# Output products of an MLP in halves of 256 columns, and the tiles of h begun 192 bytes past a multiple of 512

## The chip, the cores and the metric

The kernel runs on one core of a Trainium2 chip. The metric is device time of one execution in microseconds (us), the median of several runs.

## The reference, cut to what matters

A retention layer (attention without a softmax, with a decaying lower triangle) gives x of 2304 tokens by 512. Two MLPs follow.

```python
attn_out = _attn_ref(q, k, v)                       # 4 batches, 8 heads, 576 tokens, 64
x = attn_out.transpose(0, 2, 1, 3).reshape(2304, 512)
h = np.maximum(x @ moe_w_in, 0.0)                   # 512 -> 2048
x = (h * h) @ moe_w_out                             # 2048 -> 512
g = x @ moe2_w_gate                                 # 512 -> 1536
x = (g / (1 + np.exp(-g)) * (x @ moe2_w_val)) @ moe2_w_out
```

The change touches `(h * h) @ moe_w_out`, the output product of the first MLP.

## The kernel before, in words

**Precision.** Every operand of an MLP product is kept as two fp32r tiles, a high part and the rest. `three` (L235 to L237) issues a product as three matmuls, high·high, high·low and low·high, all added up in PSUM. Each matmul is preceded by its own load of 128 by 128 weights (LDWEIGHTS, the rows of PEld).

**Blocks of tokens.** `BLOCKS` cuts the first MLP's tokens into five blocks j of 512, 256, 512, 512 and 512. Blocks 0 and 1 (`PLAIN_BLOCKS = 2`) are computed plainly: `mlp1_h` makes one 128-row piece f of h (of 16) in the bank `hps`, `mlp1_act` makes max(h,0) squared and its two parts in a tile `h`, and `mlp1_y` multiplies that with the output weights and adds it to four PSUM tiles `acc` (e = 0 to 3). The retention of the later tokens is put between the pieces of these two blocks. Blocks 2 to 4 take the input product in Strassen's manner, two pieces f at a time (`mlp1_s`, step p of 8): seven products of 256 columns, six matmuls each, moving operand `xb`, into the banks `gv` and `hps`; between them stand the output products of the step before, as pieces `y` (one e of one f: three matmuls of 512 columns, rows acc<-h,w). A step orders its work as product 0, 1, two pieces, 2, 3, two pieces, 4, 5, two pieces, 6, two pieces. After that comes the second MLP (`mlp2_gv`, rows gv<-xc,w of 384 columns, and its output pieces, rows with 128x256 and `at`).

**Order of the work.** `Plan` writes the order of each engine's instructions from costs given by hand; an operation's cost is a number beside the function that emits it. TensorE's operations are chained in program order (`pe`). The queue of DMA issues is SP's.

**Where tiles lie.** The pools are stacked in SBUF in the order of the code; pools named `pad...` shift what follows. Before the change the pool `hp` (two slots of 4096 bytes) begins at a multiple of 512 bytes, and `shift(n)` moves a tile of h with under 512 columns, that of block 1, by 48 elements (192 bytes). The tiles x of block 1 and `xb` begin 192 bytes past a multiple of 512, as their pads have it; those of x of block 0, of `xc` and of the weights begin at a multiple of 512.

Of the kernel before, what the change touches and what calls it, by code (L numbers as in the profile page):

```python
# [10 lines left out]
F32 = mybir.dt.float32  # L11
F32R = mybir.dt.float32r
# [12 lines left out]
NF1, NF2 = F1 // 128, F2 // 128  # L25
# [11 lines left out]
PLAIN_BLOCKS = 2  # L37
# [4 lines left out]
HALF1 = 256  # L42
# [150 lines left out]
def kernel(ctx: ExitStack, tc: tile.TileContext, units, qtab, tab, w1, w2, out):  # L193
# [15 lines left out]
    wp = ctx.enter_context(tc.tile_pool(name="wp", bufs=1, side="right"))  # L209
    wstack = ExitStack()  # L210
    wa = wstack.enter_context(tc.tile_pool(name="wa", bufs=NA, side="right"))
    ctx.enter_context(tc.tile_pool(name="pad2", bufs=1)).tile([128, 224], F32, name="pad2")
    hp = ctx.enter_context(tc.tile_pool(name="hp", bufs=2))
    io = ctx.enter_context(tc.tile_pool(name="io", bufs=3))
    sp = ctx.enter_context(tc.tile_pool(name="sp", bufs=1))
    cv = ctx.enter_context(tc.tile_pool(name="cv", bufs=1))
# [16 lines left out]
    def three(ps, ws, xs, first, last, onto=False):  # L233
        (wh, wl), (xh, xl) = ws, xs
        nc.tensor.matmul(ps, lhsT=wh, rhs=xh, start=first, stop=False, skip_group_check=onto)  # L235
        nc.tensor.matmul(ps, lhsT=wh, rhs=xl, start=False, stop=False, skip_group_check=onto)  # L236
        nc.tensor.matmul(ps, lhsT=wl, rhs=xh, start=False, stop=last, skip_group_check=onto)  # L237
# [3 lines left out]
    def pe(us, fn, deps=(), fill=None):  # L241
        o = do("PE", us, fn, [*deps, pe_last[0]])
        o.fill = fill
        pe_last[0] = o
        return o
# [254 lines left out]
    def shift(n):  # L500

        return 48 if n < 512 else 0
# [178 lines left out]
    def out_cols(f, e):  # L681
        t, at = Wt[f // 2 * 2 + 1], f % 2 * 512 + e * 128
        return [t[:, a, at:at + 128] for a in range(2)]

    Hs, accs = {}, {}
# [30 lines left out]
    def mlp1_act(j, f):  # L716
        n = BLOCKS[j][1] * C
        i = at1[j, f]
        k = n / 512
        st = {}  # L720
        on_act = True

        def relu():
            st["r"] = io.tile([128, n], F32, tag="io", name="r")
            nc.scalar.activation(out=st["r"], in_=banks[0][:, :n], func=ACTF.Relu)

        def square():
            if on_act:
                nc.scalar.activation(out=st["r"], in_=st["r"], func=ACTF.Square)
            else:  # L730
                nc.vector.tensor_tensor(out=st["r"], in0=st["r"], in1=st["r"], op=ALU.mult)

        def hi():
            t = hp.tile([128, 2 * n + shift(n)], F32R, tag="h", name="h")
            Hs[j, f] = t[:, shift(n):].rearrange("p (a n) -> p a n", a=2)
            nc.scalar.copy(out=Hs[j, f][:, 0], in_=st["r"])

        def lo():
            nc.vector.tensor_tensor(out=Hs[j, f][:, 1], in0=st["r"], in1=Hs[j, f][:, 0].bitcast(F32), op=ALU.subtract)

        a = do("ACT", 0.17 + 0.43 * k, relu, [h_op[j, f], hlo_op.get(order1[i - 1]) if i else None], -3)
        relu_op[j, f] = a
        if on_act:
            b = do("ACT", 0.19 + 0.43 * k, square, [a], -2)
        else:
            b = do("DVE", 0.16 + 0.53 * k, square, [a], -2)
        c = do("ACT", 0.19 + 0.43 * k, hi, [b, y_op.get(order1[i - 2]) if i > 1 else None], -2)
        hlo_op[j, f] = do("DVE", 0.16 + 0.53 * k, lo, [c], -2, lock=True)

    io_users, io_alloc = [], []  # L750

    def mlp1_y(j, f, apart=False):

        n = BLOCKS[j][1] * C

        def go(es=range(KC)):
            ht = Hs[j, f]
            for e in es:
                if f == 0:
                    accs.setdefault(j, {})[e] = pacc.tile([128, n], F32, tag="acc", name="acc")  # L760
                three(accs[j][e], out_cols(f, e), [ht[:, a] for a in range(2)], f == 0, f == NF1 - 1)

        def piece(e):
            def emit():
                free = [acc_free[j - 1][e]] if f == 0 and j else []
                y_op[j, f] = y_op[j, f, e] = pe(3 * n * MM, lambda: go([e]), [hlo_op[j, f], *free])
                if e == KC - 1 and f == NF1 - 1:
                    mlp1_save(j)
            return emit

        if apart:
            return [piece(e) for e in range(KC)]
        if f == NF1 - 1:
            for e in range(KC):
                piece(e)()
            return
        y_op[j, f] = pe(12 * n * MM, go, [hlo_op[j, f], w1_done[f // 2 * 2 + 1], *(acc_free.get(j - 1, ()) if f == 0 else ())])
# [745 lines left out]
    for b in range(N2):  # L1523
# [13 lines left out]
        for f in range(NF2):  # L1537
# [9 lines left out]
            n = len(mine)  # L1547
# [94 lines left out]
```

## Time and profile before

| | |
|---|---|
| runs, median (lowest to highest) | 863.67 us (862.26 to 865.38), 3 runs |
| the profiled execution's own time | 866.6 us |
| its span, first to last instruction | 864.8 us |
| mean granted clock of TensorE, share of full speed | 0.996 |
| TensorE busy | 853.8 us (99%) |
| VectorE, ScalarE, GpSimd busy | 628.0, 506.7, 134.7 us |

The profile shows one execution. PE is TensorE's matmuls and PEld its weight loads, DVE is VectorE, ACT ScalarE, POOL GpSimd, SP the queue that issues DMAs. A matmul's duration runs from its start to its last result, and the next one starts before that; so the time that matmuls cost is read from start to start (called the pitch below), not from durations.

### The profile page before, as it was taken

The page shows a single profiled execution, that of the slowest core. Times are in us where ns is not written, and L with a number is a line of the kernel's source. Part 1 is how long each engine was busy: PE and PEld are TensorE (multiplying, and loading weights), DVE is VectorE, ACT ScalarE, POOL GpSimd, SP SyncE. Part 2 cuts the span into 40 slices and gives each one's busy share as a digit, 9 for nine tenths or more (in the row PEclk, how much of TensorE's full clock was granted, in tenths as well). Part 3 has the DMA queues.
Part 4 walks back from the last instruction along what each step waited for, and adds up shares of the span by engine and source line. Part 5 has one row for each costly group of instructions (what it writes and reads, how often), then busy time and mean ns, then how long its engine had stood idle before and what let it go on. Part 6 is the DMA issues. An engine that isn't in the chain of part 4 may idle for free.

```text
span 864.8 us, 15867 instructions
## 1 busy us (share of the span) xinstructions
PE 853.8 (99%) x5990; PEld 804.0 (93%) x5990; DVE 628.0 (73%) x1034; ACT 506.7 (59%) x994; POOL 134.7 (16%) x141
## 2 busy tenths in 40 slices
PE   8999999999999999999999999999999999999998
PEld 6878888989999999999998999999999999999998
DVE  5799987646677857785788778588666688656675
ACT  3577774437877877887887444365333355333353
POOL 3121127651223022212310201000000000000000
PEclk9899999999999999999999999999999999999999
DMA  9587879999989789969899898978867788776782
GB/s 369 206 329 268 305 268 315 387 379 301 316 297 329 267 288 346 315 233 329 281 342 385 300 402 296 392 259 308 318 227 263 261 261 281 276 260 223 267 265 74
DMA packets 113084, 254.83 MB, mean 295 GB/s; under 512 B 8560, under 2 KB 67696, under 8 KB 103664
## 3 DMA queue, kind: packets, MB, share of 16 engines
q1 hardware_dynamic: 113008, 253.82, 83.5%
q8 instruction: 47, 0.77, 0.4%
q14 instruction: 29, 0.24, 0.1%
HBM read 195.59 MB, written 58.20 MB: 293 GB/s over the span
## 4 chain that ended last, share of the span: by engine, by line
PE 92%; DMA 5%; ACT 1%; DVE 1%; issue 0%; SPq 0%; DVEq 0%
PE gv L235 13%; PE gv L237 13%; PE gv L236 13%; PE acc L237 7%; PE acc L236 7%; PE acc L235 7%; PE acc L1285 4%; PE acc L1287 4%; PE acc L1286 4%; PE hps L235 4%; PE hps L237 4%; PE hps L236 4%; PE sc L577 1%; DMA raw<-w 1%; DMA qk<-units 1%; DMA w<-ws 1%
## 5 line engine op out<-in xcount | busy, mean ns | idle before, releaser
L235 PE MATMUL gv<-xc,w 128*128 128x384 f32 x504 | 169.4, 336 | 0.2 <-ACT u L1133 0.2
L237 PE MATMUL gv<-xc,w 128*128 128x384 f32 x504 | 168.9, 335 | 0.0
L236 PE MATMUL gv<-xc,w 128*128 128x384 f32 x504 | 168.7, 335 | 0.0
L236 PE MATMUL acc<-h,w 128*128 128x512 f32 (+1 forms) x320 | 117.3, 367 | 0.0
L237 PE MATMUL acc<-h,w 128*128 128x512 f32 (+1 forms) x320 | 117.3, 367 | 0.0
L235 PE MATMUL acc<-h,w 128*128 128x512 f32 (+1 forms) x320 | 117.3, 367 | 0.0
L453 POOL TENSOR_TENSOR f<-f 128x256 f32<-128x256 f32 x72 | 61.9, 859 | 274.2 <-DVE cw L410 181.5
L235 PEld LDWEIGHTS gv<-xc,w 128*128 128x128 f32 x504 | 94.6, 188 | 1.3 <-ACT u L1133 0.6
L236 PEld LDWEIGHTS gv<-xc,w 128*128 128x128 f32 x504 | 94.6, 188 | 0.1
L237 PEld LDWEIGHTS gv<-xc,w 128*128 128x128 f32 x504 | 94.6, 188 | 0.0
L1287 PE MATMUL acc<-w,at 128*128 128x256 f32 x288 | 81.0, 281 | 0.0
L1285 PE MATMUL acc<-w,at 128*128 128x256 f32 x288 | 80.9, 281 | 0.0
L1286 PE MATMUL acc<-w,at 128*128 128x256 f32 x288 | 80.9, 281 | 0.0
L237 PEld LDWEIGHTS acc<-h,w 128*128 128x128 f32 x320 | 60.1, 188 | 10.0
L235 PE MATMUL gv<-xb,w 128*128 128x256 f32 x238 | 67.1, 282 | 0.0
L237 PE MATMUL gv<-xb,w 128*128 128x256 f32 x238 | 66.8, 281 | 0.0
L236 PE MATMUL gv<-xb,w 128*128 128x256 f32 x238 | 66.8, 281 | 0.0
L236 PEld LDWEIGHTS acc<-h,w 128*128 128x128 f32 x320 | 60.1, 188 | 6.4
L235 PEld LDWEIGHTS acc<-h,w 128*128 128x128 f32 x320 | 60.1, 188 | 6.4
L927 DVE TENSOR_TENSOR h<-g,h 128x256 fp32r<-128x256 f32 x96 | 47.9, 499 | 19.1 <-ACT h L923 18.2
L1145 DVE TENSOR_TENSOR m<-gv,m 128x384 f32<-128x384 f32 x36 | 20.1, 558 | 53.5 <-PE gv L237 53.5
L1133 ACT COPY m<-gv 128x384 f32<-128x384 f32 x72 | 34.5, 479 | 40.7 <-PE gv L237 40.2
(174 smaller groups left out, 2094.9 us busy)
## 6 DMA issues: line engine op xcount, KB each, us to landing
w<-wdS SPq DMA_DIRECT2D x36, 1024.0 KB, 5.5
raw<-w SPq DMA_DIRECT2D x34, 1024.0 KB, 7.5
w<-wdP SPq DMA_DIRECT2D x36, 768.0 KB, 7.3
w<-ws SPq DMA_DIRECT2D x94, 256.0 KB, 5.0
w<-wdOP SPq DMA_DIRECT2D x54, 256.0 KB, 5.4
w<-wdOS SPq DMA_DIRECT2D x18, 768.0 KB, 7.5
ws<-cw SPq DMA_DIRECT2D x16, 512.0 KB, 8.5
wdS<-cw SPq DMA_DIRECT2D x12, 512.0 KB, 6.3
```

What stands on the lines that cost most here:

```text
L235: nc.tensor.matmul(ps, lhsT=wh, rhs=xh, start=first, stop=False, skip_group_check=onto)
L236: nc.tensor.matmul(ps, lhsT=wh, rhs=xl, start=False, stop=False, skip_group_check=onto)
L237: nc.tensor.matmul(ps, lhsT=wl, rhs=xh, start=False, stop=last, skip_group_check=onto)
L453: nc.gpsimd.tensor_tensor(out=w[:, o], in0=w[:, x], in1=w[:, y], op=op)
L577: nc.tensor.matmul(s[h][:, p], lhsT=A[c][r, p, 1], rhs=A[c][r, p, 0], start=True, stop=True)
L927: nc.vector.tensor_tensor(out=t[:, 1, half], in0=st[key][:, half], in1=t[:, 0, half].bitcast(F32), op=ALU.subtract)
L1133: nc.scalar.copy(out=st[name], in_=late[bank][:, :HALF])
L1145: nc.vector.tensor_tensor(out=st["m5"], in0=late["MA"][:, :HALF], in1=st["m5"], op=ALU.add)
L1285: nc.tensor.matmul(ps, lhsT=ah, rhs=wh, start=product not in ONTO and q == 0 and off == 0, stop=False, skip_group_check=True)
L1286: nc.tensor.matmul(ps, lhsT=ah, rhs=wl, start=False, stop=False, skip_group_check=True)
L1287: nc.tensor.matmul(ps, lhsT=al, rhs=wh, start=False, stop=q == NQ - 1, skip_group_check=True)
```

## The change

Where block j is 2, 3 or 4, each output piece of three matmuls over 512 columns becomes six over 256: three for the first half of the columns, then three for the second, with the same weights, into the two halves of the same PSUM tile. And pads move the pool `hp` by 320 bytes: its tiles now begin 192 bytes past a multiple of 512, for every block; the shift inside block 1's tile is dropped, so that block 1 lies as it did, while what stands behind `hp` keeps its place. The costs that `Plan` reads stay the same.

```diff
-    ctx.enter_context(tc.tile_pool(name="pad2", bufs=1)).tile([128, 224], F32, name="pad2")
+    ctx.enter_context(tc.tile_pool(name="pad2", bufs=1)).tile([128, 144], F32, name="pad2")
     hp = ctx.enter_context(tc.tile_pool(name="hp", bufs=2))
+    ctx.enter_context(tc.tile_pool(name="pad7", bufs=1)).tile([128, 80], F32, name="pad7")
...
         def hi():
-            t = hp.tile([128, 2 * n + shift(n)], F32R, tag="h", name="h")
-            Hs[j, f] = t[:, shift(n):].rearrange("p (a n) -> p a n", a=2)
+            Hs[j, f] = hp.tile([128, 2, n], F32R, tag="h", name="h")
...
-                three(accs[j][e], out_cols(f, e), [ht[:, a] for a in range(2)], f == 0, f == NF1 - 1)
+                if j < PLAIN_BLOCKS:
+                    three(accs[j][e], out_cols(f, e), [ht[:, a] for a in range(2)], f == 0, f == NF1 - 1)
+                    continue
+                for lo in range(0, n, HALF1):
+                    half = slice(lo, lo + HALF1)
+                    three(accs[j][e][:, half], out_cols(f, e), [ht[:, a, half] for a in range(2)], f == 0 and not lo, f == NF1 - 1, True)
```

## Rows read from the trace of the kernel before

**Rows 1.** The page, first part: busy us (share of the span) and instructions.

```profile
PE 853.8 (99%) x5990; PEld 804.0 (93%) x5990; DVE 628.0 (73%) x1034; ACT 506.7 (59%) x994; POOL 134.7 (16%) x141
```

**Rows 2.** Waits of TensorE, whole span: first and last of ten.

```profile
PE hps L236 <- DVE x L649: 1.9, 1, 1.9
...
PE gv L235 <- ACT u L1133: 0.2, 1, 0.2
```

**Rows 3.** Windows by stage: us, busy time and instructions of each engine, clock, DMA.

```profile
223.50:301.00 77.50, 77.50 (x488) 70.26 (x487) 59.02 (x100) 64.31 (x141) 14.37 (x16) 1.00 0.89 304
...
379.00:457.00 78.00, 78.00 (x496) 70.91 (x495) 58.29 (x97) 62.05 (x139) 17.44 (x20) 1.00 0.88 302
457.00:475.00 18.00, 17.76 (x93) 16.15 (x93) 14.72 (x25) 12.68 (x21) 1.68 (x2) 1.00 0.98 383
```

**Rows 4.** TensorE's groups by form, started in or running into 223.52 to 456.84.

```profile
L235 PE MATMUL acc<-h,w 128*128 128x512 f32 x182 | 70.8, 389 | 0.0
...
L235 PE MATMUL gv<-xb,w 128*128 128x256 f32 x218 | 61.3, 281 | 0.0
L235 PE MATMUL hps<-xb,w 128*128 128x256 f32 x88 | 24.7, 281 | 0.0
...
L235 PE MATMUL gv<-xb,sx 128*128 128x256 f32 x2 | 0.6, 281 | 0.0
```

**Rows 5.** Timeline of TensorE: start us, us, engine, line, operation.

```profile
224.21 0.39 PE L235 MATMUL acc<-h,w 128*128 128x512 f32 x1
...
225.57 0.28 PE L235 MATMUL hps<-xb,w 128*128 128x256 f32 x1
```

**Rows 6.** The same view, end of block 1 and start of block 2.

```profile
212.44 0.28 PE L237 MATMUL acc<-h,w 128*128 128x256 f32 x1
...
218.22 0.28 PE L237 MATMUL gv<-xb,w 128*128 128x256 f32 x1
218.39 0.39 PE L235 MATMUL gv<-xb,w 128*128 128x256 f32 x1
...
219.20 0.28 PE L235 MATMUL hps<-xb,w 128*128 128x256 f32 x1
...
219.54 0.28 PE L235 MATMUL hps<-xb,w 128*128 128x256 f32 x1
```

**Rows 7.** The same view, end of block 0's last output product, block 1's first pieces.

```profile
149.28 0.39 PE L237 MATMUL acc<-h,w 128*128 128x512 f32 x1
149.51 0.28 PE L235 MATMUL hps<-x,w 128*128 128x256 f32 x1
```

**Rows 8.** The same view, retention between two pieces of block 1.

```profile
155.04 0.28 PE L237 MATMUL acc<-h,w 128*128 128x256 f32 x1
155.16 1.05 PE L604 MATMUL xs<-qt,state 128*128 128x128 f32 x8
...
158.72 0.38 PE L235 MATMUL hps<-x,w 128*128 128x256 f32 x1
...
159.53 0.28 PE L235 MATMUL hps<-x,w 128*128 128x256 f32 x1
...
160.21 0.28 PE L235 MATMUL acc<-h,w 128*128 128x256 f32 x1
```

**Rows 9.** Timeline of VectorE in a step of block 2.

```profile
245.23 0.42 DVE L901 TENSOR_TENSOR g<-hps,m 128x256 f32<-128x256 f32 x1 [0.76 <-PE hps L237]
```

**Rows 10.** Timeline of TensorE in the same step.

```profile
247.03 0.28 PE L235 MATMUL hps<-xb,w 128*128 128x256 f32 x1
```

**Rows 11.** The queue's waits: us in total, times, longest.

```profile
SPq L1098 <- PE gv L237: 207.4, 67, 7.8
SPq L841 <- PE gv L237: 50.6, 50, 6.0
```

**Rows 12.** The chain that ended last, at the start of the second MLP.

```profile
458.09 0.02 ACT m L1133
...
463.08 0.39 ACT u L1133
```

**Rows 13.** TensorE's groups by form, whole span.

```profile
L237 PE MATMUL gv<-xc,w 128*128 128x384 f32 x504 | 168.9, 335 | 0.0
...
L1287 PE MATMUL acc<-w,at 128*128 128x256 f32 x288 | 81.0, 281 | 0.0
...
L237 PE MATMUL acc<-h,w 128*128 128x256 f32 x64 | 17.7, 277 | 0.0
```

**Rows 14.** Timeline of TensorE in the second MLP's last quarter.

```profile
770.93 0.28 PE L1285 MATMUL acc<-w,at 128*128 128x256 f32 x1
...
772.30 0.34 PE L235 MATMUL gv<-xc,w 128*128 128x384 f32 x1
```

## The prediction

> **What bounds the kernel now.** I read the page first: TensorE is busy for 853.8 of 864.8 us, VectorE for 628.0 [rows 1]. Then what TensorE waits for: ten waits in the whole span, none over 1.9 us, the last of them 0.2 us at the start of the second MLP [rows 2]. Then the windows, since an average over stages can hide one with another limit: in blocks 2 to 4, the stretch that the change is about, TensorE is busy for the whole of 77.5 and 78 us at a granted clock of 1.00 (its upper level, 2.4 GHz), with DVE at about 59 and ACT at about 64 [rows 3]. So in this stretch the time is the number of matmuls times their pitch, and nothing else. Last the timeline, to get pitches, because this is where the surprise lies.
>
> The reader is to see two pitches for one and the same kind of matmul. The six 512-column matmuls from 224.21 to 225.57 take 1.36 us, 226.7 ns each [rows 5]. In the stretch from 223.52 to 456.83, three lines with 182 of them each make 546; the 256-column ones on `xb` are three lines of 218 on gv, of 88 on hps, and 12 with `sx` (two triples on gv as shown, two on hps), 930 in all [rows 4]. 233.31 us less 546 x 226.7 ns leaves 109.5 us, or **117.8 ns** each. But just ahead of it, from 212.44 to 218.22, 51 matmuls of 256 columns follow one another, block 1's output pieces and block 2's first `xb` products mixed, in 5.78 us: **113.3 ns** each, exactly half of a 512-column one [rows 6]. Same shapes, same weights pool, same clock: 4.5 ns differ.
>
> What came before decides which pitch it is. Behind the last 512-column matmul of block 0 the 48 matmuls of block 1 from 149.51 on run 47 steps to 155.04, 117.7 ns each [rows 7, 8]. Then the retention work comes between; the first matmul after it takes twice its time, the pitch settles within six, and from 159.53 to 160.21 six take 0.68 us, 113.3 ns [rows 8]. A pause at 218.22 does the same: behind it the pitch is at 113.3 again from 219.20 on [rows 6]. So a 512-column matmul with its operand at a multiple of 512 sets the slow pitch, the slow pitch then keeps itself up, and a pause clears it. Since 223.52, where block 2's first 512-column piece starts, one such piece stands in every step, and the slow pitch never leaves.
>
> **The change, part by part.**
>
> *The halves.* 576 matmuls (4 e, 16 f, 3 blocks, 3 each) become 1152 of half the length: at 113.3 ns the pair takes 226.6 ns against 226.7, no change; at 117.8 ns it takes 235.6, 8.9 more. Each brings a weight load; at the 113.3 ns of rows 6 every matmul has one of its own, so that it lies hidden under the matmul before it. If that cover were gone the pitch would rise; the nearest row to that is the slow 117.8.
>
> A rule of the Trainium skill speaks against the split: the page TensorE: Matmul & The Clock Gate, section Back-to-back issue gap, gives N / 2.4 + 2.5 ns, so a fixed 2.5 ns for every matmul. By it 576 more of them would cost 1.4 us (an estimate from that page), and a 256-column one would always take the same. The rows disagree with both: two at 113.3 make one at 226.7 [rows 5, 6], which leaves no fixed part, and there are two pitches.
>
> *What the halves remove.* From block 2 on no 512-column matmul is left until the second MLP. Block 2 is entered at the fast pitch [rows 6]; what interrupts it there, pauses, leads back to the fast one. Then the 930 `xb` matmuls run at 113.3: 930 x 4.5 = **4.2 us less**. Bounds: 0 (all stay at 117.8) to 4.2.
>
> *The 192 bytes.* For blocks 2 to 4 they put the halves of h where `xb` and block 1's h lie, whose mix ran at 113.3 [rows 6]. In block 0 192 matmuls of 512 columns now begin there too, a form that the trace doesn't have. A gain is excluded, as 226.7 is already twice the fastest 256-column pitch; a loss is bounded by the slow surcharge, 192 x 4.5 = 0.9 us. I take 0, since at 256 columns this place shows the fast pitch. If the place and not the length is what sets the slow pitch, block 1's 48 slow matmuls gain 48 x 4.4 = 0.2 us more.
>
> *Behind the stretch.* The last 30 pieces' matmuls run among the 384-column ones of the second MLP, where the slow pitch rules (below): 30 x 8.9 = 0.3 us more at most; I take 0.2.
>
> *Does the gain reach the end?* Three things could be late when TensorE comes 4 us sooner. The evictions inside a step: VectorE's add for product 4 runs 245.23 to 245.65 and its bank is next written at 247.03 [rows 9, 10], 1.4 us of room, against 27 ns that each product gets shorter. The loads: SP waits for TensorE to free their places, 207.4 us in all at L1098 and 50.6 at L841 [rows 11]; they are set off by TensorE and come sooner with it. And ACT at the start of the second MLP, the one place where the chain leaves TensorE: from 458.09 to 463.47 it runs through ACT [rows 12]. But that piece begins with the copy of the second MLP's own first product, so it moves along whole. DMA is at 0.98 of its time there [rows 3]; I count no loss, and up to 1 us for the range. Nothing is moved past a queue: `Plan` reads the same costs, so the order of every engine is the old one.
>
> The sum: -4.2 + 0.2 = -4.0 us. Against the profiled execution, 864.8 us of span and 1.8 around it, 866.6 - 4.0 = 862.6. That execution is 2.9 above the median of the runs, so the median becomes 863.67 - 4.0 = **859.7 us**.
>
> **Rivals.**
>
> *Slower: the slow pitch stays.* If the pitch is slow for another reason than the 512-column pieces, say the alternation of banks or of products with y pieces, the 930 gain nothing and 576 pairs pay 8.9 ns: +5.1 us, 868.8. For it: output pieces of the second MLP, all 256 columns, average 281 ns of duration, block 1's 277, so they are slow there nearly throughout [rows 13] though no 512-column matmul is near. Against it: they stand among 384-column ones, and rows 6 show the very mix of blocks 2 to 4 running fast. It decides where more than 46% of the stretch's 2022 short matmuls (930 and 1092) are slow: all of them slow cost 9.1 us, now 4.2 are paid.
>
> *The pitch changes back and forth.* If something besides pauses and long matmuls sets the slow pitch now and then, a third to a half of the matmuls stay slow: -1.2 to +0.4 us, 862.5 to 864.0, within 0.3% (2.6 us, about what a measurement of this kernel can tell from no change). Waits that eat the gain at the second MLP end there too.
>
> *A cost per matmul.* If each of the 576 extra matmuls pays something of its own, the rows bound it at 0 (two at 113.3) and 8.9 ns (two at 117.8). It takes 576 times that from the 4.0: at a third of the upper bound, 3 ns, -2.3 us remain, 861.4; from 7 ns on nothing does. Against it stands that 226.7 is twice 113.3. This is the rule of the Trainium skill named above (TensorE: Matmul & The Clock Gate, Back-to-back issue gap), by which alone, with no gain on `xb`, the time would be 863.67 + 1.4 = 865.1.
>
> *More: the second MLP gets fast too.* If the fast pitch lives on there, its output pieces, x288 on three lines on acc alone [rows 13], would save 864 x 4.5 = 3.9 us more: 855.8. Once they do run fast, from 770.93 to 772.30, 12 in 1.37 us [rows 14]. Against it: the 384-column matmuls before it set the slow pitch as the long ones do.
>
> **How the numbers follow.** The forecast 0.65, the slow pitch 0.12, back and forth 0.11, a cost per matmul 0.07, more 0.05. The forecast alone spans 858.6 (the 0.2 of block 1, and 0.9 for the spread of the runs) to 861.6 (0.9 in block 0, 1 behind the stretch). The range leaves out the slow rival whole (0.12) and most of "more" (0.04): 857.2 to 866.0, the upper end being back and forth with a spread of 1.9 us for the runs. Faster by over 0.3%: 0.60 of the forecast, all of "more", a third of the cost per matmul: 0.67. Within 0.3%: the rest of the forecast, of the cost and of back and forth: 0.20. Slower: the slow rival and 0.01 of back and forth: 0.13.
>
> **What the profile would show.** Right: durations of gv<-xb and hps<-xb near 277 instead of 281, 1152 more short acc<-h rows at 277, about 229 us from the first output piece of block 2 to the first gv<-xc, and TensorE without a new wait. Wrong: xb at 281 and acc<-h with it (slow); pitches that switch inside the stretch; hps<-x and acc<-h of block 0 above 389 ns (place); or a wait of TensorE at the second MLP that grew by microseconds.

## The result, and the profile after

The changed kernel takes **868.95 us** (median of 9 runs, 866.07 to 872.75) against 863.78 for the kernel before beside it; the ratio is 1.0067, 95% interval [1.0052, 1.0082]. It is slower, by about the 5.1 us of the rival *the slow pitch stays*. Its profiled execution took 871.61 us, with a span of 869.8 against 864.8.

The page first, its busy part, then the waits of TensorE (us in total, times, longest), then two windows by stage:

```profile
PE 858.2 (99%) x6566; PEld 829.4 (95%) x6566; DVE 626.1 (72%) x1034; ACT 507.5 (58%) x994; POOL 135.6 (16%) x141
```

```profile
PE hps L237 <- DVE x L650: 1.9, 1, 1.9
...
PE gv L236 <- ACT u L1138: 0.3, 1, 0.3
```

```profile
223.50:301.00 77.50, 77.50 (x660) 77.48 (x659) 56.47 (x98) 63.46 (x140) 16.18 (x19) 1.00 0.90 307
379.00:457.00 78.00, 78.00 (x664) 78.00 (x663) 57.02 (x96) 60.85 (x136) 17.56 (x20) 1.00 0.84 283
```

The 576 extra matmuls are there. The longest wait of TensorE is still 1.9 us [rows 2], and none falls between the first output piece of block 2 and the second MLP. The clock is at its upper level, and blocks 2 to 4 are still TensorE alone [rows 3]. So the loss is pitch again. The groups by form and the timeline say which:

```profile
L237 PE MATMUL acc<-h,w 128*128 128x256 f32 x448 | 125.5, 280 | 0.0
...
L1290 PE MATMUL acc<-w,at 128*128 128x256 f32 x288 | 80.3, 279 | 0.0
...
L237 PE MATMUL gv<-xb,w 128*128 128x256 f32 x238 | 66.8, 281 | 0.0
...
L237 PE MATMUL acc<-h,w 128*128 128x512 f32 x64 | 25.2, 394 | 0.0
```

```profile
134.62 0.39 PE L236 MATMUL acc<-h,w 128*128 128x512 f32 x1
...
136.95 0.39 PE L237 MATMUL acc<-h,w 128*128 128x512 f32 x1
...
225.06 0.33 PE L236 MATMUL gv<-xb,w 128*128 128x256 f32 x1
225.22 0.28 PE L237 MATMUL gv<-xb,w 128*128 128x256 f32 x1
...
225.81 0.28 PE L236 MATMUL acc<-h,w 128*128 128x256 f32 x1
...
226.52 0.28 PE L236 MATMUL acc<-h,w 128*128 128x256 f32 x1
...
463.96 0.34 PE L236 MATMUL gv<-xc,w 128*128 128x384 f32 x1
```

Three things are to be seen.

- Block 0: ten steps from 134.62 to 136.95 are 2.33 us, 233 ns for each 512-column matmul at 192 bytes, where it was 226.7 [rows 5]: 6.6 ns each, 192 x 6.6 = **1.3 us**.
- Blocks 2 to 4: at 225.06 TensorE pauses (0.16 us to the next start); behind it six halves take 0.71 us, 118 ns each, with no matmul of 512 columns in the 74 us before. From the first piece to the first gv<-xc it is 238.15 us against 233.3 [rows 4]: **4.8 us** more.
- The second MLP gives some back: acc<-w,at averages 279 ns of duration against 281 [rows 13], since long spells of it ran fast. From the first gv<-xc to the end it is 405.8 us, before 864.8 - 456.84 = 408.0: **2.1 us** less.

The first piece of block 2 starts 2.3 us later than before (225.81 against 223.52), 1.3 of it block 0; that makes 2.3 + 4.8 - 2.1 = 5.0, the span. The other 1.0 us of the later start was not followed up. Executions differ by more than that there: in the traces of e4 to e9 the piece starts between 221.4 and 224.2 us.

### The profile page after: what moved, and what is told of

It reads as the page before. It is cut to its first block, busy times and chain, and to the rows that moved or that the text cites. A ratio compares the mean times of both kernels' runs of the same rounds, so it can differ in the third digit from the quotient of the medians.

```text
span 869.8 us, 17020 instructions
## 1 busy us (share of the span) xinstructions
PE 858.2 (99%) x6566; PEld 829.4 (95%) x6566; DVE 626.1 (72%) x1034; ACT 507.5 (58%) x994; POOL 135.6 (16%) x141
## 4 chain that ended last, share of the span: by engine, by line
PE 93%; DMA 4%; ACT 1%; DVE 1%; issue 0%; SPq 0%; DVEq 0%
PE gv L236 13%; PE gv L238 13%; PE gv L237 13%; PE acc L237 8%; PE acc L238 8%; PE acc L236 8%; PE hps L236 4%; PE acc L1290 4%; PE acc L1292 4%; PE acc L1291 4%; PE hps L238 4%; PE hps L237 4%; PE sc L578 1%; DMA raw<-w 1%; PE xs L605 1%; DMA qk<-units 1%
## 5 line engine op out<-in xcount | busy, mean ns | idle before, releaser
L237 PE MATMUL acc<-h,w 128*128 128x256 f32 (+1 forms) x512 | 150.8, 294 | 0.0
L238 PE MATMUL acc<-h,w 128*128 128x256 f32 (+1 forms) x512 | 150.8, 294 | 0.0
L236 PE MATMUL acc<-h,w 128*128 128x256 f32 (+1 forms) x512 | 150.7, 294 | 0.0
L236 PEld LDWEIGHTS acc<-h,w 128*128 128x128 f32 x512 | 97.7, 191 | 2.8
L238 PEld LDWEIGHTS acc<-h,w 128*128 128x128 f32 x512 | 96.1, 188 | 2.9
L237 PEld LDWEIGHTS acc<-h,w 128*128 128x128 f32 x512 | 96.1, 188 | 2.8
```

## The experiments

Each timed kernel has its own runs of the kernel before on the same chip.

**Halves without the place (e1).** h lies where it lay before; the products of blocks 2 to 4 are cut. The diff is against the changed kernel.

```diff
-    ctx.enter_context(tc.tile_pool(name="pad2", bufs=1)).tile([128, 144], F32, name="pad2")
+    ctx.enter_context(tc.tile_pool(name="pad2", bufs=1)).tile([128, 224], F32, name="pad2")
     hp = ctx.enter_context(tc.tile_pool(name="hp", bufs=2))
-    ctx.enter_context(tc.tile_pool(name="pad7", bufs=1)).tile([128, 80], F32, name="pad7")
...
-            Hs[j, f] = hp.tile([128, 2, n], F32R, tag="h", name="h")
+            t = hp.tile([128, 2 * n + shift(n)], F32R, tag="h", name="h")
+            Hs[j, f] = t[:, shift(n):].rearrange("p (a n) -> p a n", a=2)
```

> The halves without the 192 bytes: h of blocks 0, 2, 3 and 4 begins at a multiple of 512 as before, the products of blocks 2 to 4 come as two matmuls of 256. Theory P (the pauses decide: a stream of 256-column matmuls can run at 113.3 or at 117.8 ns, whatever lies at 192 bytes, and keeps the pitch in which the last pause left it; the place costs only matmuls of 512 columns, 6.6 ns each): block 0 is back at 226.7 ns, 1.3 us better than after; the halves and xb of blocks 2 to 4 share one pitch, either 117.8 (then about 867.6, before + 3.8) or 113.3 (then about 858.6, before - 5). Rival Q (the place of h decides: halves at 192 bytes run slow and drag xb along, halves at a multiple of 512 run at 113.3 and let xb go fast): 113.3 throughout, 859.7 or less. Rival R (each extra matmul costs something of its own): xb stays at 117.8 or drops to 113.3 while the halves keep 117.8 by themselves.

Measured: 866.94 us against 863.70, ratio 1.0038 [1.0022, 1.0054]. Neither theory: block 0 is back at 226.7 ns, but in blocks 2 to 4 two pitches alternate inside every step, 118.4 ns on h and 115.1 on `xb` (means over 20 us from starts). That is 1092 x 5.1 + 930 x 1.8 = 7.2 us above 113.3, against the 4.2 paid before: +3.0. In the trace the stretch is 3.1 us longer than before, and the runs are 3.2 apart. So the place does matter for 256 columns, and a multiple of 512 is a bad one.

**The place without the halves (e2).**

```diff
-                if j < PLAIN_BLOCKS:
-                    three(accs[j][e], out_cols(f, e), [ht[:, a] for a in range(2)], f == 0, f == NF1 - 1)
-                    continue
-                for lo in range(0, n, HALF1):
...
+                three(accs[j][e], out_cols(f, e), [ht[:, a] for a in range(2)], f == 0, f == NF1 - 1)
```

> The 192 bytes without the halves: h begins 192 bytes past a multiple of 512 in every block, products stay one matmul of 512 columns. Theory P: block 0 as in the changed kernel, 192 x 6.6 ns = 1.3 us; in blocks 2 to 4 576 matmuls of 512 columns at 233.3 instead of 226.7 ns cost 3.8 us, xb stays at 117.8: about 868.8, the same as the changed kernel with halves, since 2 x 117.8 is nearly 233.3. Rival Q (the place matters for short matmuls and not for the length): the 512-column ones at 226.7 in blocks 2 to 4, xb slow, 1.3 us more than before at most: 865.

Measured: 864.18 against 863.70, ratio 1.0004 [0.9986, 1.0021]; P's 868.8 was a miss. The trace tells why. Groups of one line, 227 to 325 us and then 340 to 457:

```profile
L236 PE MATMUL gv<-xb,w 128*128 128x256 f32 x96 | 27.0, 281 | 0.0
...
L236 PE MATMUL gv<-xb,w 128*128 128x256 f32 x106 | 29.4, 277 | 0.0
```

h is at 232.4 ns throughout, 5.7 above 226.7, but `xb` drops from 117.8 to 113.8 ns at 325.2 us, behind a slip of 30 ns (0.15 us from one start to the next), and stays there:

```profile
325.10 0.28 PE L238 MATMUL hps<-xb,w 128*128 128x256 f32 x1
325.22 0.31 PE L236 MATMUL gv<-xb,w 128*128 128x256 f32 x1
325.37 0.28 PE L237 MATMUL gv<-xb,w 128*128 128x256 f32 x1
```

Beside 512-column matmuls at 192 bytes the fast pitch can live; in the trace of the kernel before, at 0, it never did. The traced execution took 866.39, 2.2 above the median, with the first 100 us of its stretch slow; how long the others were fast is not known.

**The changed kernel again (e3).**

> The changed kernel once more, for its trace: P expects that the pitch of blocks 2 to 4 is one of 113.3 and 117.8 for long spells, and that the point from which it is slow can move from execution to execution; Q expects 117.8 throughout and the same spells of the second MLP as in the first trace.

Measured: one execution of 864.49 us, span 862.7. It is the same program as the first trace, and it runs the whole stretch fast:

```profile
224.81 0.32 PE L236 MATMUL gv<-xb,w 128*128 128x256 f32 x1
224.97 0.28 PE L237 MATMUL gv<-xb,w 128*128 128x256 f32 x1
...
225.55 0.28 PE L236 MATMUL acc<-h,w 128*128 128x256 f32 x1
...
226.45 0.28 PE L238 MATMUL acc<-h,w 128*128 128x256 f32 x1
...
454.71 0.34 PE L236 MATMUL gv<-xc,w 128*128 128x384 f32 x1
```

```profile
379.00:457.00 78.00, 78.00 (x684) 78.00 (x683) 59.40 (x97) 62.54 (x141) 17.35 (x20) 1.00 0.89 312
```

Eight steps from 225.55 to 226.45 are 0.90 us, about 113 ns each; 684 matmuls start where the first trace has 664. From the first piece to the first gv<-xc it is 229.16 us, 4.1 less than before: the forecast's -4.2, in one execution. The pause ahead of it looks the same as in the first trace, 0.16 us from start to start, but here it is followed by 113 ns and there by 118. The timeline rounds; the start times in ns, as the trace holds them, give 157 ns here and 167 there. Eight traces (this one, the first, e4 to e9) have this pause and the same matmuls behind it: 157 ns with the fast pitch behind it once, 162 to 167 ns with the slow pitch seven times. With one fast case and no run that sets the length, this is a hint and not a cause.

**The place by itself (m1).** The core of the kernel, run over a list of sections:

```python
xh, xl = m[:, off:off + cols], m[:, 1024 + off:1024 + off + cols]
o = ps[:, :cols]
for n in range(14):
    wh, wl = (w[:, a, at + n % 8 * 128:at + n % 8 * 128 + 128] for a in range(2))
    nc.tensor.matmul(o, lhsT=wh, rhs=xh, start=n == 0, stop=False)
    nc.tensor.matmul(o, lhsT=wh, rhs=xl, start=False, stop=False)
    nc.tensor.matmul(o, lhsT=wl, rhs=xh, start=False, stop=n == 13)
nc.vector.tensor_copy(out=s[:, :min(width, cols)], in_=ps[:, :min(width, cols)])
```

> Not the reference's work: sections of 42 matmuls in triples (high and low parts), each with its own weight load, into one bank, entered through a pause in which VectorE copies 64, 150 or 256 columns of the bank. 512, 256 and 384 columns; the moving operand 0, 64, ... 448 bytes past a multiple of 512, weights at 0; then weights at 192 and 320 bytes with the moving operand at 0 and 192. P: 256 columns run at 113.3 or 117.8 at every place, and which of the two depends on the pause; 512 columns at 226.7 with both at 0 and at 233.3 where the places differ. Q: 256 columns at 113.3 where the places agree and at 117.8 where they differ, the same after every pause.

Pitches, each the mean of the last 25 in a section, from starts. The place is the moving operand's address less the weights', modulo 256 bytes; sections with the same difference agree, whether the moving operand or the weights are moved.

| place, bytes | 256 columns | 384 columns | 512 columns |
|---|---|---|---|
| 0 | 120.0 | 173.3 | **226.7** |
| 64 | 117.8 | 173.3 | 228.9 |
| 128 | 118.6 | 175.5 to 176.0 | 232.1 to 233.5 |
| 192 | **113.3** (7 sections) or 117.8 (2) | 173.3 (4 of 6) to 176.7 | 233.4 |

The copy that closes a section is the pause ahead of the next. Rows of four sections: 256 columns at 0, at 192 behind a copy of 256 columns, at 192 behind one of 64; 512 columns at 192.

```profile
279.38 0.28 PE L46 MATMUL ps<-m,w 128*128 128x256 f32 x1
...
281.06 0.28 PE L45 MATMUL ps<-m,w 128*128 128x256 f32 x1
```

```profile
330.11 0.28 PE L47 MATMUL ps<-m,w 128*128 128x256 f32 x1
...
331.76 0.28 PE L46 MATMUL ps<-m,w 128*128 128x256 f32 x1
```

```profile
335.84 0.28 PE L46 MATMUL ps<-m,w 128*128 128x256 f32 x1
...
337.20 0.28 PE L46 MATMUL ps<-m,w 128*128 128x256 f32 x1
```

```profile
125.25 0.39 PE L47 MATMUL ps<-m,w 128*128 128x512 f32 x1
...
127.59 0.39 PE L45 MATMUL ps<-m,w 128*128 128x512 f32 x1
```

14 steps in 1.68 us, 14 in 1.65, 12 in 1.36, 10 in 2.34. Of P this holds: at 192 bytes 256 columns have two pitches and keep the one in which a pause left them. Its "at every place" falls: at 0, 64 and 128 every pause left one pitch, 117.8 to 120.0. Q falls: 256 columns are slowest where the places agree, and at 192 the pitch is not the same after every pause. The best place for 512 columns is the worst for 256.

**Block 0 back to its place (e4).**

```diff
-    ctx.enter_context(tc.tile_pool(name="pad2", bufs=1)).tile([128, 144], F32, name="pad2")
+    ctx.enter_context(tc.tile_pool(name="pad2", bufs=1)).tile([128, 16], F32, name="pad2")
...
-            Hs[j, f] = hp.tile([128, 2, n], F32R, tag="h", name="h")
+            t = hp.tile([128, 1088], F32R, tag="h", name="h")
+            at = 16 if n == 512 else 0
+            Hs[j, f] = t[:, at:at + 2 * n].rearrange("p (a n) -> p a n", a=2)
```

> The changed kernel, with h of block 0 alone moved 64 bytes further (256 bytes past a multiple of 512, where m1 gives 226.7 ns for 512 columns, as at 0); halves stay at 192. Expected by the first theory as m1 leaves it (512 columns pay 6.6 ns each at 192 bytes; 256 columns at 192 bytes run at 113.3 or 117.8, and the last pause decides which): block 0 at 226.7, 192 x 6.6 = 1.3 us less than the changed kernel: about 867.7 while blocks 2 to 4 are slow, about 863.2 in executions in which they are fast. Rival (the shift costs nothing in block 0 and the surplus of the changed kernel lies in the stretch alone): 868.9, as the changed kernel.

Measured: ten executions in two groups with nothing between: 858.56, 860.61, 861.07, 862.11, 862.83 and 868.38, 868.95, 869.20, 869.38, 870.72; before 863.64. The traced one, 868.95, has 117.8 ns throughout the stretch, and block 0 at 226.7. The two medians, 861.1 and 869.2, lie 8.1 us apart; 2022 short matmuls by 4.5 ns are 9.1. The 1.3 us of block 0 show in the trace and not in the times: the long group is no shorter than the changed kernel's 868.95 in its own runs.

**What switches the pitch (m2, m3).**

> Not the reference's work: again sections of triples behind pauses of 64, 100, 150 or 200 columns. First 256 columns with the moving operand 128 to 240 bytes past a multiple of 512 in steps of 4 to 16 bytes, then 384 columns there; then 30 matmuls of 256 columns at 192 bytes, one triple of another size (64 to 512 columns, at 192 or at 0), and 30 more of 256; then mixtures of 256 with 512 columns at 0 and at 192 and with 384. If only exactly 192 bytes can run at 113.3, its neighbours run at 115 to 119; if there is a place that is fast after every pause, it is the better place for the halves. What my prediction said (a 512-column matmul at a multiple of 512 sets the slow pitch): the 30 behind a 512-column triple at 0 run at 117.8 after either pause, those behind 64 to 384 columns keep the pitch they had. Rival (any triple of another length or place can switch it, as a pause can): some of the shorter ones switch too, and not all of the 512.

m2: only exactly 192 bytes reached 113.3; 188 gave 115.5 to 120.0 and 196 about 120, and no place was fast after every pause. At 192 the pause behind a copy of 150 columns came out slow (683 ns from the last start to the next); in m1 it came out fast three times, at 682 and 683 ns. In m1 the pause behind 256 columns came out slow twice and fast once, at 797 ns each. So it is not the length of the pause alone.

> Not the reference's work: sections that make the pitch slow with a triple of 512 columns at 0 (which did so in each of ten cases of m2), run 9 to 12 matmuls of 256 columns at 192 bytes, then one candidate (a triple of 64, 128, 160, 192, 224, 320 or 384 columns at 192, of 384 or 256 at 0, a pair 192 + 320 or 128 + 384, 512 at 192), 12 of 256, the candidate again, 12 of 256. Then mixtures as in the second MLP, entered slow: 4 triples of 384 columns at 0, 160 or 192 bytes and 1 to 3 triples of 256 in turn. If a triple of another length always lands in the same pitch, a candidate is a switch: 128, 192 and 320 would lead to 113.3 from both sides, 64 and 512 to 117.8. If what follows depends on the state before, the candidates keep 117.8 where they begin slow.

m3 asked what one triple between runs of 256 columns does. Pitch ahead of it and behind, cases counted:

| the triple | behind 113.3 | behind 117.8 |
|---|---|---|
| 512 columns at 0 | 34 of 34 slow | 9 slow, 11 fast |
| 512 at 192; 160; 64; the pair 192 + 320 | 12 of 12 slow | 12 of 12 fast |
| 128, 192, 224 at 192; 256 at 0 | 15 of 15 fast | 9 of 9 fast |
| 320 at 192; 384 at 0 | no case | 12 of 12 slow |
| 384 at 192; the pair 128 + 384 | 7 of 7 fast | 5 of 5 fast |

So what follows depends on the triple and on the state before. That 512 columns at 0 set the slow pitch is true from the fast side, and from the slow side they often do the opposite. Four triples of 384 at 0 led to 113.3 in 36 of 36, though the second MLP of the kernel before runs its output pieces at 117.8 among just such ones: there this rule did not carry over.

The pitch is not the whole state either. Behind the slow pitch, the triple of 512 at 0 led to the fast one in all 11 cases in which it ran at 233 to 236 ns itself, and left the slow one in all nine in which it ran at 226 to 228. m2 has cases against the table: behind the slow pitch, 512 at 192 stayed slow once, and 384 at 0 led to the fast one once. And two triples in a row differ from one: in m2 two of 512 at 192 left the fast pitch behind them in eight of eight, as the pairs of e2 do, and two of 512 at 0 left the slow one, as in the kernel before.

**One product decides (e5, e6, e7, then e8, e9).** All are e4 with single products cut otherwise; each has one of the `edges` lines. What the expectations call steps 1, 2 and 3 of block 2 are its pieces f = 1, 2 and 3.

```diff
-                for lo in range(0, n, HALF1):
-                    half = slice(lo, lo + HALF1)
+                edges = (0, CUT, HALF1, n) if j == PLAIN_BLOCKS and f in (1, 2, 3) and e == 0 else (0, HALF1, n)   # CUT: 64 in e5, 192 in e6
+                edges = {(2, 1, 0): (0, 128, 512)}.get((j, f, e), (0, HALF1, n))                        # e8
+                edges = {(2, 1, 0): (0, 128, 512), (2, 2, 0): (0, 512)}.get((j, f, e), (0, HALF1, n))   # e9
+                for lo, hi in zip(edges, edges[1:]):
+                    half = slice(lo, hi)
```

> e4, and in steps 1, 2 and 3 of block 2 the first product's first half is cut into 64 and then 192 columns. By m3 a triple of 192 leads to 113.3 ns from either pitch, so all that follows to the end of block 4 should be fast in every execution: the five short executions of e4 (858.6 to 862.8, median 861.1) plus 3 cuts x 0.22 us (64 columns 29 + 110 + 112 ns, 192 columns 86 + 113 + 112, against 340) = 861.7, and none above 866. Rival (something else of an execution than the last odd triple decides, say memory or what the DMAs do): two groups of times 8 us apart as in e4, median near 866.

> The same three halves, cut into 192 and then 64 columns: the same instructions in number and size, only their order is turned. By m3 64 columns behind a fast triple lead to 117.8, so the stretch should be slow in every execution: the five long executions of e4 (868.4 to 870.7, median 869.2) plus 0.7 = 869.9, none under 866. Rival: the same as the one with 64 first.

e5: 861.07 against 864.73, ratio 0.9974 [0.9952, 0.9995]; e6: 861.21, ratio 0.9967 [0.9950, 0.9983]. e6 was expected slow and is fast. In its trace 192 and then 64 columns lead from 117.8 to 113.3; in the traced execution of e5, its one long one (870.33), 64 and then 192 leave 117.8 as it was, three times. In the trace of e7 (below) the same cut leads from 117.8 to 113.3 at once. m3 had tested each with whole 256-column triples around it; two odd ones in a row behave otherwise, and these runs settle nothing about the rule.

In e7 the output pieces of the second MLP get a cut as well:

```diff
+            edges = (0, 64, 256) if (product, q, t) == ("P1", NQ - 1, 1) else (0, 256)
+            for lo, hi in zip(edges, edges[1:]):
+                p, xh, xl = ps[:, lo:hi], wh[:, lo:hi], wl[:, lo:hi]
...
```

> e5, and in each of the three batches of the second MLP one output piece at the head of the long run of pieces is cut into 64 and 192 columns too. If the runs of pieces (some 480 matmuls between 573 and 596, 700 and 717, 838 and 862 us) keep 113.3 from there, they give back up to 480 x 4.45 ns = 2.1 us for 3 x 0.22 = 0.7: 860.3. If the 113.3 does not last there, 862.4.

e7: 863.30, ratio 0.9978 [0.9963, 0.9994], 3.0 above the expected. In its trace the runs of output pieces behind two of the three cuts stay at 117.8, and the third was at 113.3 ahead of its cut. A miss. The traced execution is e7's one long one (869.24), and its stretch shows why: it is fast up to the start of block 3, where TensorE waits for VectorE.

```profile
323.38 0.28 PE L238 MATMUL acc<-h,w 128*128 128x256 f32 x1
...
324.74 0.28 PE L238 MATMUL hps<-xb,w 128*128 128x256 f32 x1
325.37 0.39 PE L236 MATMUL gv<-xb,w 128*128 128x256 f32 x1 [0.36 <-DVE g L909]
...
325.83 0.28 PE L236 MATMUL gv<-xb,w 128*128 128x256 f32 x1
...
326.89 0.28 PE L236 MATMUL acc<-h,w 128*128 128x256 f32 x1
```

Twelve steps ahead of the pause take 1.36 us, 113 ns; nine behind it 1.06, 118, and so it stays to the end of block 4. The stretch is 236.0 us, 5.2 more than in e6's trace, where the same wait (0.47 us from start to start) ended fast. So a pause inside the stretch can lose what a cut at its start has set.

> e4 with one product of block 2's step 1 cut 128 + 384 instead of 256 + 256, with plain halves around it, as the candidate stood in m3. There 128 + 384 led to 113.3 from either pitch in six of six, so that every execution should run fast from about 227 us to the end of block 4: the short executions of e4 (median 861.1) plus 0.2 (865 ns for the triples of 128 and 384 against 680) = 861.3. Rival (the pitch of an execution is not set by the last odd triple): two groups, as in e4.

> e8, and one product of the next step left whole, 512 columns at 192 bytes. In m3 such a triple led from 113.3 to 117.8 in four of four. So every execution should be slow from that step to the end of block 4: the long executions of e4 (median 869.2) plus 0.2 = 869.4. Rival: the same times as e8.

e8: **861.65** against 865.74, ratio 0.9956 [0.9936, 0.9976]; ten of twelve executions lie between 859.8 and 863.5, one at 865.4, one at 869.6. e9: **869.63**, ratio 1.0052 [1.0034, 1.0069], six executions from 868.7 to 872.6 (of the four cases that its expectation counts in m3, one is m2's). One product of 192 in blocks 2 to 4 differs between the two, and it moves the whole by 8.0 us. The switches stand in the timelines, e8's first:

```profile
227.62 0.28 PE L238 MATMUL acc<-h,w 128*128 128x256 f32 x1
227.74 0.22 PE L236 MATMUL acc<-h,w 128*128 128x128 f32 x1
227.80 0.27 PE L237 MATMUL acc<-h,w 128*128 128x128 f32 x1
227.91 0.28 PE L238 MATMUL acc<-h,w 128*128 128x128 f32 x1
228.02 0.39 PE L236 MATMUL acc<-h,w 128*128 128x384 f32 x1
...
228.60 0.28 PE L236 MATMUL acc<-h,w 128*128 128x256 f32 x1
...
229.62 0.28 PE L236 MATMUL gv<-xb,w 128*128 128x256 f32 x1
```

```profile
230.11 0.28 PE L236 MATMUL gv<-xb,w 128*128 128x256 f32 x1
...
230.79 0.39 PE L236 MATMUL acc<-h,w 128*128 128x512 f32 x1
231.01 0.40 PE L237 MATMUL acc<-h,w 128*128 128x512 f32 x1
231.25 0.39 PE L238 MATMUL acc<-h,w 128*128 128x512 f32 x1
231.48 0.28 PE L236 MATMUL acc<-h,w 128*128 128x256 f32 x1
...
232.30 0.28 PE L237 MATMUL gv<-xb,w 128*128 128x256 f32 x1
```

In e8 nine steps behind the cut take 1.02 us, 113 ns, where 118 stood ahead of it. In e9 the six ahead of the whole product take 0.68 us, 113 ns; behind it seven take 0.82, 117 ns. Both pitches then last: windows of e8, then of e9, each to the same 229 or 238 us of stretch as e3 and the first trace.

```profile
379.00:457.00 78.00, 78.00 (x684) 78.00 (x683) 58.80 (x97) 62.75 (x141) 17.42 (x20) 1.00 0.90 315
```

```profile
379.00:457.00 78.00, 78.00 (x664) 78.00 (x664) 57.19 (x95) 61.05 (x136) 17.56 (x20) 1.00 0.86 292
```

e5, e6, e7 and e8 come out faster than the kernel before in their own runs, with intervals below 1, e8 by 4.1 us. e8's rule (every execution fast) holds for ten of twelve.

## Why the prediction was wrong

- **The step that failed** is "Block 2 is entered at the fast pitch [rows 6]; what interrupts it there, pauses, leads back to the fast one." It took the pauses of rows 6 and 8, which all ended fast, for a rule. A pause ends in either pitch: at 225.06 in the first trace it ended slow, at 224.81 in e3 fast, with the same program. In both traces it then stays to the end of block 4, so one pause at the start decides 2022 x 4.5 ns = 9 us; in e7 a pause at 325 us ended slow as well. "A pause clears it" should have been a chance: in e4 five of ten executions were short, and of the changed kernel's nine timed ones eight took 868.35 us or more.
- **"A 512-column matmul with its operand at a multiple of 512 sets the slow pitch"** holds from the fast side (m3, 34 of 34), and in m2 two such triples in a row, as the kernel before has them, left the slow pitch behind them in eight of eight. But it is not the only cause, so taking those matmuls away did not remove the slow pitch, it made it a matter of chance. The rival's reason for (output pieces of the second MLP, slow with no such matmul near) was the right warning, and was given 0.12; the signs named for it, `xb` and acc<-h both at 281, are what the first trace shows (its row of acc<-h has 280, with block 1's fast ones among them).
- **The size of the gain** was right where the mechanism ran: -4.2 forecast, -4.1 in e3's stretch; e8, with block 0 put back and 0.2 paid for its cut, gained 4.1 in all against the forecast's 4.0. So was the size of the loss: +5.1 for the rival, +4.8 in the stretch of the first trace.
- **The 192 bytes in block 0** were mis-sized: taken as 0, bounded by 0.9 (192 x 4.5), measured 1.3 (192 x 6.6). The bound carried the surcharge of a 256-column matmul over to a 512-column one; m1 gives 233.4 against 226.7 for it. The sign named for it, acc<-h of block 0 above 389 ns, is there with 394.
- **The halves as such** cost nothing: two at 113.3 make 226.7. The rule of the Trainium skill (TensorE: Matmul & The Clock Gate, Back-to-back issue gap), N / 2.4 + 2.5 ns, gives 109.2 and 215.8 for 256 and 512 columns, an estimate from that page. The same section gives the rule for a single matmul by itself, a condition that the prediction left out, and about 131 ns at 512 columns where each has its weight load. No section of m1 shows any of these, and the pitch at one size moves by up to 6% with the place alone, which the rule doesn't contain.
- **The gain reaches the end**: right. In e3 and e8 it is 408.0 us from the first gv<-xc to the end, as before (862.7 - 454.71; 861.7 - 453.69), so nothing behind the stretch takes the gain back. In these two no wait of TensorE appeared in the stretch. In the traces of e6 and e7, fast up to 324 us, one did, for VectorE's g at the start of block 3 (0.2 and 0.4 us); the prediction had looked at the additions inside a step alone.
- *The second MLP* sped up by 2.1 us in the first trace and by nothing in e3, so it too depends on the execution.

What stays open: why two pitches exist, what a pause must be like to end in one or the other, why e8 had one long execution (it was not traced), whether the times between the groups (866.18 in e6, 865.41 in e8, 866.07 of the changed kernel) come from a pause in mid-stretch as in e7's trace, and why the second MLP keeps 117.8 where m3's mixtures ran at 113.3.

## What to carry to other kernels

When the same matmul shows two pitches in one trace, look for what each spell began with, and trace a second execution before calling anything the cause: a state that keeps itself up can be set by an accident at its start. Where such a state is worth microseconds, don't remove one of its causes; put in something that sets it, as the 128 + 384 cut does in most executions, and look for the pauses behind it that can undo it. And before moving a tile or cutting a product, measure that size at that place: here the best place for 512 columns was the worst for 256.

## What the runs showed of the hardware

- The pitch of fp32r matmuls with a weight load each depends on the moving operand's address less the weights', modulo 256 bytes (m1): 113.3 to 120.0 ns for 256 columns, 226.7 to 233.5 for 512. The best place for 512 columns (0) is the worst for 256, and the best for 256 (192) is among the worst for 512.
- At 192 bytes 256 columns have two lasting pitches, 113.3 and 117.8 ns; in e2 the change from slow to fast stands at a slip of 30 ns, in e7 that from fast to slow at a pause of 0.64 us. Each lasted for some 225 us of unbroken work (e8, e9).
- In a triple of 64 to 224 columns the second and third matmul take 107 to 115 ns to the next start, whatever their columns (m3); so 128 + 384 in place of 256 + 256 costs 0.2 us a product (0.86 us from 227.74 to 228.60 in e8, against 0.68).
